# Moving the first reciprocals, the constants and the decode differences, and starting the expert products in unit 7

## The chip, the cores and the metric

The kernel runs on one core of a Trainium2 chip. A core has five engines that run their own queues in order and wait for one another by semaphores: TensorE (PE in the profile, with its weight loads as PEld), VectorE (DVE), ScalarE (ACT), GpSimd (POOL) and SyncE (SP), whose queue issues the DMAs here. The metric is the device time of one execution in microseconds, lower is better.

## The reference

Three layers follow one another on 2304 tokens (4 batches of 576) of width 512, in float32.

```python
# attention: B=4, H=8, S=576, D=64; c = cumsum(max(s, 0))
scores = q @ k.T / 8 + min(-(c_i - c_j), 0), causal      # per batch and head
attn = exp(scores - rowmax) / (rowsum + 1e-9)
x = concat_heads(attn @ v)                               # 2304 x 512
# first expert layer, d_ff = 768
x = max(max(x @ w1, x @ w2), x @ w3) @ w_out
# second expert layer, d_ff = 2048, g a rational function
h = x @ w_in
g = (a0 + a1 h + a2 h^2 + a3 h^3) / (1 + |b0| |h| + |b1| h^2 + 1e-6)
out = g @ w_out2
```

## The kernel before

**Precision.** Matmul operands of the expert layers are split into two parts: hi, a rounded copy made by ScalarE, and lo, the difference to the full value. A product is the sum of hi·hi, hi·lo and lo·hi (`mm3`, line 65): three passes over the 128-row slices, the lo weights in the last pass.

**Decode.** A 512 KB slice of a weight matrix is loaded raw, and `decode_steps` (line 416) makes hi and lo of it in five operations: three on VectorE (lines 419 to 421), which shuffle bits of the raw slice into a buffer `x` of which there is one; a cast on ScalarE to hi (line 422); and the difference on GpSimd to lo (line 423), which reads `x` and hi. The next slice's first operation writes `x` again. There are 46 such jobs: 18 slices of w1, w2, w3 (named by column group 0 to 5 and matrix 0 to 2, so (4,0) is the 13th), then 28 slices of the other weights, called sp, which are decoded in place and stored to DRAM for later ("spilled").

**Attention in units.** `units` (line 236) lists 32 units, each four heads (a group g) and one or two row tiles x. A unit passes through these stages, one or two units behind one another:
- `scores` (line 267): for four heads, three matmuls each that run side by side on 32 rows (two halves of the head dimension, then the bias). VectorE adds the mask, scales and takes the row minimum (line 291), ScalarE takes the exponential with its row sum (line 297). The last row tile (x = 3) comes in two halves.
- `norm` (line 302): VectorE adds 1e-9 to the row sums and takes reciprocals (lines 306 and 307), GpSimd multiplies each head's rows by them (line 313). `scores` schedules it two steps later.
- `transposes` of the unit before (line 328): TensorE turns the weights round, ScalarE and, for the second bank, VectorE copy them out of PSUM (lines 356 and 358).
- `pv` of two units before (line 362): the products with v; ScalarE copies the hi part of x (line 394), VectorE makes the lo part (line 395).

Score and transpose banks come from one ring of five PSUM banks.

**Fills.** As soon as a block of 384 tokens is through `pv` for all heads, its 18 expert groups (6 column groups by 3 matrices) are appended to `moe1_todo`. `fill` (line 470) issues the next one if the slice that it needs is entered in `w13`; if not, it issues nothing, and the step is spent. A group is 12 matmuls (line 72); ScalarE copies the result of matrix 0 (line 453), VectorE takes the maximum with the other two (line 455). Groups left at the end of attention run behind it.

**Order.** In this part of the program each engine's queue has the order in which the code issues. The main loop (line 541) makes a list of steps for unit u: scores, transposes, scores' second half, transposes, pv, with the fills spread between them (none before unit 8; then 3, or 4 when more than 18 groups are open or after unit 27). `step` (line 252) issues one of them, counts `now` up, takes background steps from `bg` (at least 5 behind scores) and issues what `after` has put into `late` when its step count is reached. Behind a step the loop also takes one operation from `prep`: the four VectorE transposes that turn a group's raw k and q (line 199); in unit 0 the last two of group 1, in units 7, 8, 14, 16 and so on those of a new group. A decode job is queued as `w_store`, `w_load` and `first` (line 505), and `first` puts the five operations at the head of `bg`. Line 544 gives the number of jobs that are begun by unit u:

```python
while njobs < min(len(jobs), u + max(0, u + 2 - U0) * 2 // 3):
    w_job()
```

With U0 = 8 that is 7 by unit 7, then 9, 11, 12, 14, 16, 17, 19, 21. A slice is entered in `w13` four steps behind its last decode operation's place.

**Start.** Before the loop, VectorE makes small constants `pc` from the partition number (lines 151 to 162), a selection matrix (lines 167 to 171), the scan of s (line 188), the first transposes of k and q, and from two matmuls (line 220) the tile `hx` and the bias row `cx` (line 224). GpSimd fills the mask (line 173), whose memory holds the scratch values of which `pc` is made.

After the loop come the remaining expert groups, then the second part of the kernel (lines 613 to 770), in which the spilled slices come back and the other products run.

Of the kernel before, what the change touches and what calls it, by code (L numbers as in the profile page):

```python
# [8 lines left out]
F32 = mybir.dt.float32  # L9
# [3 lines left out]
ALU = mybir.AluOpType  # L13
# [5 lines left out]
def kernel(  # L19
# [20 lines left out]
    nc = tc.nc  # L40
# [9 lines left out]
    BIG = 1000000000.0  # L50
    scale = 1.0 / float(D) ** 0.5
# [7 lines left out]
    NG = N // 4  # L59
# [40 lines left out]
    MS = 448  # L100
    mask = at.tile([128, MS], F32, name="mask")
# [7 lines left out]
    def xtile(shape, dt, name):  # L109
        return p1.tile(list(shape), dt, tag="x", bufs=3, name=name)  # L110
# [18 lines left out]
    def load_v(g):  # L129
# [12 lines left out]
    first_raw = at.tile([128, 4, S], F32, tag="PT", bufs=2, name="raw1").rearrange("p a s -> p (a s)")  # L142
    load_qk(1)

    pc = at.tile([128, 4 + 2 * NG], F32, name="pc")
    pi_ = mask.bitcast(U32)[:, 0:4 + 2 * NG]
    nc.gpsimd.iota(pi_[:, 0:1], pattern=[[0, 1]], base=0, channel_multiplier=1)
# [3 lines left out]
    nc.vector.tensor_scalar(pi_[:, 3:4], pi_[:, 0:1], 2, 7, ALU.logical_shift_right, ALU.bitwise_and)  # L153
    pf = mask[:, 32:36 + 2 * NG]
    nc.vector.tensor_copy(pf[:, 0:4 + NG], pi_[:, 0:4 + NG])
    nc.vector.tensor_copy(pc[:, 0:1], pf[:, 1:2])
    nc.vector.tensor_scalar(pc[:, 1:2], pf[:, 1:2], -2.0, 1.0, ALU.mult, ALU.add)
    nc.vector.tensor_scalar(pc[:, 2:3], pf[:, 2:3], -1.0, 1.0, ALU.mult, ALU.add)
    nc.vector.tensor_copy(pc[:, 3:4], pf[:, 2:3])
    nc.vector.tensor_scalar(pf[:, 12:12 + NG], pf[:, 4:4 + NG], pf[:, 3:4], None, ALU.is_equal)  # L160
    nc.vector.tensor_scalar(pc[:, 4:4 + NG], pf[:, 12:12 + NG], pf[:, 2:3], -1.0, ALU.mult, ALU.mult)
    nc.vector.tensor_tensor(pc[:, 4 + NG:4 + 2 * NG], pf[:, 12:12 + NG], pc[:, 4:4 + NG], ALU.add)

    wsel = xtile([128, 3, 128], F32, "wsel")
    sel, n_i = wsel[0:N, 0, :], wsel.bitcast(U32)[0:N, 1:3, :]
# [4 lines left out]
    nc.vector.tensor_copy(sel, n_i[:, 0, :])  # L170
    nc.vector.tensor_scalar(sel, sel, pf[0:N, 0:1], None, ALU.is_equal)

    nc.gpsimd.memset(mask, 0.0)
    nc.gpsimd.affine_select(
        out=mask[:, MS - 128:MS], in_=mask[:, MS - 128:MS], compare_op=ALU.is_ge,
        fill=-BIG / scale, base=0, pattern=[[-1, 128]], channel_multiplier=1)
    make_identity(nc, ident)
    for y in range(2):
        nc.gpsimd.memset(P[y][:, :, PW - 64:PW], 0.0)
# [6 lines left out]
    c = sc[:, 1, :]  # L186
    nc.vector.tensor_scalar(sc[:, 0, :], sc[:, 0, :], 0.0, 1.0 / scale, ALU.max, ALU.mult)
    nc.vector.tensor_tensor_scan(c, sc[:, 0, :], sc[:, 0, :], 0.0, ALU.add, ALU.max)


    qk_t = {}
# [21 lines left out]

    p0, p1_ = prep_qk(0), prep_qk(1)
    hx = xtile([128, 2, S], F32R, "hx")
    p0.pop(0)()
    for y in range(2):
        y0, y1 = y * S // 2, (y + 1) * S // 2
# [6 lines left out]
    for f in p0 + p1_[0:2]:  # L225
# [7 lines left out]
    USC = [[[(0, 0, 64, 0), (1, 0, 192, 64)]], [[(2, 0, 320, 0)]], [[(3, 0, 448, 0)]],  # L233
           [[(4, 0, 288, 0)], [(4, 288, 576, 0)]]]
# [14 lines left out]
    def after(lag, fn):  # L249
        late.append((now + lag, fn))  # L250

    def step(fn, *a):
        nonlocal now
        fn(*a)
        now += 1
        for _ in range(max(-(-len(bg) // bg_steps[0]), 5 if fn is scores else 0)):
            if bg:
                bg.pop(0)()
        bg_steps[0] = max(1, bg_steps[0] - 1)
        for x in [x for x in late if x[0] <= now]:  # L260
            late.remove(x)
            x[1]()

    bg = []
    bg_steps = [1]

    def scores(u, y):
        g, x = units[u]
        Pu, sm = P[u % 2], smalls[u % 3]
        kt, qt, et = qk_t["k", g], qk_t["q", g], qk_t["e", g]  # L270
        pss = [st_tile(f"sc{u}_{y}_{h}") for h in range(4)]
        for t, j0, j1, o in USC[x][y]:
            r0, nr = IT[t]
            for z in range(3):
                for h in range(4):
                    r = slice(32 * h, 32 * h + 32)
                    if z < 2:
                        l, rr = qt[r, z, r0:r0 + nr], kt[r, z, j0:j1]
                    else:
                        l, rr = et[r, r0:r0 + nr], bias_r[r, j0:j1]  # L280
                    nc.tensor.matmul(pss[h][0:nr, o:o + j1 - j0], l, rr, start=(z == 0), stop=(z == 2),  # L281
                                     tile_position=(32 * h, 0))
        for t, j0, j1, o in USC[x][y]:
            r0, nr = IT[t]
            W = r0 + nr
            base = pbase(t)
            m0 = j0 + (MS - W if nr == 128 else MS - 128) if j1 == W else 0
            last = j1 == W
            k = 4 * (t == 0)
            for h in range(4):  # L290
                nc.vector.tensor_tensor_reduce(  # L291
                    Pu[0:nr, h, base + j0:base + j1], pss[h][0:nr, o:o + j1 - j0], mask[0:nr, m0:m0 + j1 - j0], -scale,
                    3.0e38 if j0 == 0 else sm[0:nr, 3, h:h + 1], ALU.add, ALU.min,
                    sm[0:nr, 0 if last else 3, k + h:k + h + 1])
                if last:
                    o_ = Pu[0:nr, h, base:base + W]
                    nc.scalar.activation(out=o_, in_=o_, func=ACTF.Exp, bias=sm[0:nr, 0, k + h:k + h + 1], scale=-1.0,  # L297
                                         accum_out=sm[0:nr, 1, k + h:k + h + 1])
        if y == len(USC[x]) - 1:
            after(2, lambda: norm(u))  # L300

    def norm(u):
# [136 lines left out]
    w13 = {}  # L439
# [48 lines left out]
    jobs = [("w13", divmod(i, 3)) for i in range(3 * KF1)] + [("sp", x) for x in range(len(spill))]  # L488
    raws = []
    stores = []  # L490
    nj = [0]

    def w_store():
        if stores:
            o, r = stores.pop(0)
            dma.dma_start(out=o, in_=r)
# [8 lines left out]
    def w_job():  # L505

        bg.append(w_store)
        bg.append(w_load)

        def first():  # L510
            kind, x, raw = raws.pop(0)
            xx = new_wx(f"{kind}{x}")
            if kind == "w13":
                t = wslot(f"w13_{x[0]}_{x[1]}")
                args = raw, xx, t[:, 0, :], t[:, 1, :], t.bitcast(F32)[:, 0, :]
            else:
                r = raw.rearrange("p f t -> p (f t)").rearrange("p (a f) -> p a f", a=2)
                args = raw, xx, r.bitcast(F32R)[:, 0, :], r.bitcast(F32)[:, 1, :], r.bitcast(F32)[:, 0, :]
            for x_, f in enumerate(decode_steps(*args)):
                bg.insert(x_, f)  # L520
            if kind == "w13":
                bg.insert(5, lambda: after(4, lambda: w13.__setitem__((x[1], x[0]), t)))
            else:
                bg.insert(5, lambda: stores.append((w2_dram[x], r.bitcast(F32))))

        bg.append(first)

# [8 lines left out]
    U0 = 8  # L536
    nblk = 0
    njobs = 0
    prep = p1_[2:4]
    loads = []  # L540
    for u in range(NU + 2):
        g, x = units[min(u, NU - 1)]
        if u >= 1:
            while njobs < min(len(jobs), u + max(0, u + 2 - U0) * 2 // 3):
                w_job()
                njobs += 1
        nfill = 0 if u < U0 else 4 if len(moe1_todo) > 18 or u > 27 else 3
        work = []
        if u < NU:
            work += [(scores, u, 0), 1]  # L550
        if 1 <= u <= NU:
            nb = len(tr_banks(units[u - 1][1]))
            work += [(transposes, u - 1, range(2)), 1]
        if u < NU and len(USC[x]) > 1:
            work += [(scores, u, 1), 1]
        if 1 <= u <= NU:
            work.append((transposes, u - 1, range(2, nb)))
        if u >= 2:
            z = (units[u - 2][0] // 2) * S + sum(IT[UT[units[u - 2][1]][-1]])
            assert not any(t[0] <= (z - 1) // TB - 3 for t in moe1_todo)  # L560
            work.append((pv, u - 2))
        work.append(1)
        nf = sum(w == 1 for w in work)
        nfill = min(nfill, len(moe1_todo))
        seq = []
        for w in reversed(work):
            if w == 1:
                kf = -(-nfill // nf)
                nfill -= kf
                nf -= 1  # L570
                seq += [(fill, 1)] * kf
            else:
                seq.append(w)
        bg_steps[0] = len(seq)
        for i, f in enumerate(reversed(seq)):
            step(*f)
            if prep:
                prep.pop(0)()
            elif loads:
                loads.pop(0)()  # L580
        while bg:
            bg.pop(0)()
        while prep:
            prep.pop(0)()
        if u >= 2 and units[u - 2][0] % 2:
            while (nblk + 1) * TB <= z:
                moe1_todo += [(nblk, fc, m) for fc in range(KF1) for m in range(3)]
                nblk += 1
        if u == 1:
            load_qk(2)  # L590
        if u < NU and x == NX - 1 and g + 2 < NG:
            prep = prep_qk(g + 2)
            bias_l(g + 2)
            if g + 3 < NG:
                loads.append(lambda g=g: load_qk(g + 3))
        if u >= 2:
            g, x = units[u - 2]
            if x == NX - 1 and g + 2 < NG:
                load_v(g + 2)
# [50 lines left out]
    for x in range(ng):  # L650
# [4 lines left out]
        while not right and done < len(direct) and done * (ng - 6) <= (x - 5) * len(direct):  # L655
            kind, c = direct[done]
# [144 lines left out]
```

## Time and profile before

| | us |
|---|---|
| median of 3 runs | 945.13 (943.19 to 945.21) |
| profiled execution, its own time | 945.91 |
| its span, first to last instruction | 944.1 |
| TensorE busy | 902.2 (96%) |
| VectorE busy | 652.4 (69%) |
| ScalarE busy | 480.4 (51%) |
| GpSimd busy | 355.3 (38%) |

The page gives the busy time of each engine, its course in 40 slices, the DMA queues, the chain of work that ended last, and the costliest groups of instructions. A row of the timeline reads: start in us, duration of the row, engine, line of the kernel, operation, tile written and tiles read, shapes, count; in square brackets the time that the engine had stood idle before it, and what released it. Rows of the same kind that follow one another are merged. TensorE's durations overlap, since a matmul's end is modelled.

### The profile page before, as it was taken

The numbers are of one execution on the slowest core, as the hardware profiler recorded it, in microseconds if no ns is written. First come the engines' busy times: TensorE is split into PE (matmuls) and PEld (weight loads), VectorE is DVE, ScalarE is ACT, GpSimd is POOL, SyncE is SP. The second block draws the span as 40 slices with busy tenths as digits, with TensorE's granted clock in tenths as the row PEclk, the third lists the DMA queues.
The fourth block names the chain that finished last, engine by engine and source line by source line (L and its number), as shares of the span: only waits on it lengthen the run. The fifth ranks groups of instructions, "written<-read, shape, count | busy, mean of one in ns | idle before, by whom it ended". The sixth has DMA issues, their size and how long they took to land.

```text
span 944.1 us, 16698 instructions
## 1 busy us (share of the span) xinstructions
PE 902.2 (96%) x6148; PEld 808.2 (86%) x6148; DVE 652.4 (69%) x1439; ACT 480.4 (51%) x1122; POOL 355.3 (38%) x424
## 2 busy tenths in 40 slices
PE   3878999999999998999999999999999999999997
PEld 2557887898789897999999999999899989999995
DVE  7677667755676665455369859849866885885985
ACT  3655445544454443322256656546645664663764
POOL 1553443433334323132035435524533552452552
PEclk9999999999999999999999999999999999999999
DMA  8224533664467454296730020002002001000000
GB/s 248 69 68 148 157 92 116 206 210 138 151 205 212 160 171 161 85 337 201 249 134 1 1 85 1 0 1 84 1 1 84 1 1 56 29 1 1 34 1 33
DMA packets 63937, 92.90 MB, mean 98 GB/s; under 512 B 22864, under 2 KB 49488, under 8 KB 63856
## 3 DMA queue, kind: packets, MB, share of 16 engines
q1 hardware_dynamic: 63856, 91.84, 30.5%
q8 instruction: 48, 0.79, 0.4%
q14 instruction: 33, 0.27, 0.1%
HBM read 65.35 MB, written 26.48 MB: 97 GB/s over the span
## 4 chain that ended last, share of the span: by engine, by line
PE 70%; DVE 13%; POOL 7%; ACT 6%; DMA 2%; issue 2%; POOLq 0%; ACTq 0%; SPq 0%; DVEq 0%
PE m L72 21%; PE hp L72 15%; PE acc L736 14%; PE mo L72 7%; PE pv L382 5%; PE sc L281 4%; PE tr L344 4%; POOL q L706 3%; POOL q L705 2%; DVE P L291 2%; DVE q L719 2%; ACT a L717 1%; DVE t_q L199 1%; DVE t_k L199 1%; DVE t L721 1%
## 5 line engine op out<-in xcount | busy, mean ns | idle before, releaser
L72 PE MATMUL m<-x,w 128*128 128x384 f32 x1296 | 245.0, 341 | 2.1 <-DVE hs L455 1.2
L72 PEld LDWEIGHTS m<-x,w 128*128 128x128 f32 x1296 | 222.0, 188 | 12.4 <-issue 6.2
L736 PE MATMUL acc<-ws,g 128*128 128x512 f32 x864 | 217.6, 394 | 1.5 <-ACT g L722 1.5
L705 POOL TENSOR_SCALAR q<-a,cf 128x384 f32<-128x384 f32 x96 | 92.9, 968 | 289.8 <-ACT a L703 274.7
L736 PEld LDWEIGHTS acc<-ws,g 128*128 128x128 f32 x864 | 160.9, 188 | 31.0 <-ACT g L722 2.4
L313 POOL TENSOR_SCALAR P<-P,small 128x192 f32<-128x192 f32 (+4 forms) x160 | 83.2, 540 | 150.4 <-DVE small L307 130.8
L72 PE MATMUL hp<-x,w2i 128*128 128x384 f32 x720 | 134.8, 336 | 0.0
L72 PEld LDWEIGHTS hp<-x,w2i 128*128 128x128 f32 x720 | 126.6, 188 | 4.3
L297 ACT ACTIVATE P<-P,small 64x64 f32<-64x64 f32 (+4 forms) x160 | 87.9, 551 | 53.0 <-DVE small L291 52.9
L706 POOL TENSOR_TENSOR q<-q,a 128x384 f32<-128x384 f32 x96 | 104.3, 1086 | 8.0
L707 DVE TENSOR_TENSOR t<-hp,t 128x384 f32<-128x384 f32 x96 | 53.0, 552 | 57.9 <-ACT t L704 57.9
L717 ACT ACTIVATE a<-q,cf 128x384 f32<-128x384 f32 x96 | 59.3, 618 | 64.2 <-POOL q L706 64.0
L719 DVE SCALAR_TENSOR_TENSOR q<-q,cf,a 128x384 f32<-128x384 f32 x96 | 72.9, 759 | 18.0 <-ACT a L718 17.4
L344 PE MATMUL tr<-ident,P 128*128 128x128 f32 (+2 forms) x480 | 67.3, 280 | 16.6 <-POOL P L313 9.9
L722 ACT CAST g<-t 128x384 fp32r<-128x384 f32 x96 | 49.2, 513 | 65.4 <-DVE t L721 65.4
L72 PE MATMUL mo<-h,wr 128*128 128x384 f32 x432 | 79.9, 336 | 0.0
L344 PEld LDWEIGHTS tr<-ident,P 128*128 128x128 f32 (+2 forms) x480 | 54.6, 140 | 28.6 <-POOL P L313 16.3
L455 DVE TENSOR_TENSOR hs<-m,hs 128x384 f32<-128x384 f32 x72 | 39.7, 553 | 55.9 <-PE m L72 50.1
L281 PE MATMUL sc<-t_k,t_q 32*128 32x288 f32 (+4 forms) x768 | 67.2, 435 | 10.9 <-DVE t_q L199 9.0
L72 PEld LDWEIGHTS mo<-h,wr 128*128 128x128 f32 x432 | 75.6, 188 | 1.5
L291 DVE CUSTOM_DVE_ANT_0 P<-sc,mask 64x64 f32<-64x64 f32 (+4 forms) x160 | 58.8, 423 | 19.3 <-PE sc L281 19.3
L703 ACT ACTIVATE a<-hp 128x384 f32<-128x384 f32 x96 | 46.8, 488 | 36.8 <-PE hp L72 36.8
(318 smaller groups left out, 1221.4 us busy)
## 6 DMA issues: line engine op xcount, KB each, us to landing
ws<-w_dram SPq DMA_DIRECT2D x18, 512.0 KB, 4.7
h_dram<-hs SPq DMA_DIRECT2D x36, 192.0 KB, 4.1
h<-h_dram SPq DMA_DIRECT2D x36, 192.0 KB, 3.4
rb<-in_moe_w_in_dram SPq DMA_DIRECT2D x10, 512.0 KB, 5.5
wr<-w_dram SPq DMA_DIRECT2D x10, 512.0 KB, 8.0
out_dram<-o SPq DMA_DIRECT2D x18, 256.0 KB, 2.5
v<-in_v_dram SPq DMA_DIRECT2D x32, 128.0 KB, 3.9
raw_k<-in_k_dram SPq DMA_DIRECT2D x7, 576.0 KB, 3.9
```

The lines of the kernel that those rows point to most:

```text
L72: nc.tensor.matmul(ps, l, r, start=(i == 0), stop=(i == len(seq) - 1))
L281: nc.tensor.matmul(pss[h][0:nr, o:o + j1 - j0], l, rr, start=(z == 0), stop=(z == 2), tile_position=(32 * h, 0))
L291: nc.vector.tensor_tensor_reduce(Pu[0:nr, h, base + j0:base + j1], pss[h][0:nr, o:o + j1 - j0], mask[0:nr, m0:m0 + j1 - j0], -scale, 3.0e3 ...
L297: nc.scalar.activation(out=o_, in_=o_, func=ACTF.Exp, bias=sm[0:nr, 0, k + h:k + h + 1], scale=-1.0, accum_out=sm[0:nr, 1, k + h:k + h + 1])
L313: nc.gpsimd.tensor_scalar(o, o, sm[0:nr, 2, k + h:k + h + 1], 0.0, ALU.mult, ALU.add)
L344: nc.tensor.transpose(ps[0:w, o:o + nr], Pu[0:nr, h, i:i + w], ident[0:nr, 0:nr])
L705: nc.gpsimd.tensor_scalar(qq, a, cf[:, 5:6], cf[:, 4:5], ALU.mult, ALU.add)
L706: nc.gpsimd.tensor_tensor(qq, qq, a, ALU.mult)
L707: nc.vector.tensor_tensor(t, h, t, ALU.mult)
L717: nc.scalar.activation(out=a, in_=qq, func=ACTF.Ln, bias=cf[:, 6:7], scale=1.0)
L719: nc.vector.scalar_tensor_tensor(qq, qq, cf[:, 6:7], a, ALU.add, ALU.mult)
L736: nc.tensor.matmul(acc[n, tt], g[:, ga, ts], w[:, wb, :], start=(fc == 0 and x == 0), stop=(fc == KF2 - 1 and x == 2))
```

## The change

- The seven small operations that make `pc`, and GpSimd's fill of the mask, are issued behind the scan.
- The second key transpose of group 0 is issued ahead of the `hx` operations.
- `scores` takes at least 6 background steps instead of 5.
- `norm(0)` is issued in unit 0, behind the remaining `prep` transposes, instead of two steps later; the other units keep `after(2, ...)`.
- The difference, last of the five decode operations, is taken out of the list. Behind the fourth, a function `run` is put into `late` for one step later and into `flush`, which the next `w_store` empties if it comes first. `run` issues the difference and enters the slice in `w13` two steps later, or queues the store of a spilled slice.
- In unit 7, when its `pv` has completed the first block, three fill steps are added.

```diff
+    p0.pop(0)()
     p0.pop(0)()
     for y in range(2):
...
-        for _ in range(max(-(-len(bg) // bg_steps[0]), 5 if fn is scores else 0)):
+        for _ in range(max(-(-len(bg) // bg_steps[0]), 6 if fn is scores else 0)):
...
-        if y == len(USC[x]) - 1:
+        if y == len(USC[x]) - 1 and u:
             after(2, lambda: norm(u))
...
     def w_store():
+        for f in list(flush):
+            f()
         if stores:
...
-            for x_, f in enumerate(decode_steps(*args)):
+            steps = decode_steps(*args)
+            end = steps.pop()
+
+            def run():
+                if run not in flush:
+                    return
+                flush.remove(run)
+                end()
+                if kind == "w13":
+                    after(2, lambda: w13.__setitem__((x[1], x[0]), t))
+                else:
+                    stores.append((w2_dram[x], r.bitcast(F32)))
+
+            steps.append(lambda: (after(1, run), flush.append(run)))
+            for x_, f in enumerate(steps):
                 bg.insert(x_, f)
-            if kind == "w13":
-                bg.insert(5, lambda: after(4, lambda: w13.__setitem__((x[1], x[0]), t)))
-            else:
-                bg.insert(5, lambda: stores.append((w2_dram[x], r.bitcast(F32))))
...
             step(*f)
+            if u == 0:
+                while prep:
+                    prep.pop(0)()
+                norm(0)
             if prep:
...
+        if u == U0 - 1:
+            for _ in range(3):
+                step(fill, 1)
```

## Rows read from the trace of the kernel before

**Rows 1.** The page: busy us of each engine, share, instructions.

```profile
PE 902.2 (96%) x6148; PEld 808.2 (86%) x6148; DVE 652.4 (69%) x1439; ACT 480.4 (51%) x1122; POOL 355.3 (38%) x424
```

**Rows 2.** Timeline of the start: VectorE's two gaps and the second key transpose.

```profile
7.55 0.52 DVE L222 TENSOR_SCALAR hx<-c,pc 128x288 f32<-128x288 f32 x1 [0.70 <-ACT hx L221]
...
8.51 0.52 DVE L222 TENSOR_SCALAR hx<-c,pc 128x288 f32<-128x288 f32 x1 [0.44 <-ACT hx L221]
8.95 1.25 DVE L199 STREAM_TRANSPOSE t_k<-raw_k 128x576 f32<-128x576 f32 x1
```

**Rows 3.** Timeline of units 0 to 2: VectorE, ScalarE and GpSimd.

```profile
17.25 2.33 DVE L199 STREAM_TRANSPOSE t_q<-raw 128x576 f32<-128x576 f32 x2
...
18.81 0.19 ACT L297 ACTIVATION_READ_ACCUMULATOR P<-P,small 128x1 f32 x1
...
25.32 0.19 ACT L297 ACTIVATION_READ_ACCUMULATOR P<-P,small 128x1 f32 x1
25.33 5.81 POOL L313 TENSOR_SCALAR P<-P,small 128x192 f32<-128x192 f32 x16 [18.52 <-DVE small L307]
...
33.15 0.42 DVE L419 TENSOR_SCALAR w13(0, 1)x<-w13(0, 1)r 128x512 uint32<-128x512 uint32 x1
```

**Rows 4.** Timeline of units 6 to 8: normalisation, x product, first fill.

```profile
66.13 3.10 POOL L313 TENSOR_SCALAR P<-P,small 128x576 f32<-128x576 f32 x4
...
66.93 0.30 PE L344 MATMUL tr<-ident,P 128*64 128x128 f32 x1 [3.12 <-POOL P L313]
...
78.67 0.27 ACT L394 CAST x<-pv 128x128 fp32r<-128x128 f32 x1
...
79.72 2.35 PE L72 MATMUL m<-x,w 128*128 128x384 f32 x12
```

**Rows 5.** Stretches: length, busy us of PE, PEld, DVE, ACT, POOL, clock, DMA.

```profile
70.00:72.00 2.00, 2.00 (x15) 1.38 (x17) 2.00 (x4) 0.17 (x1) 0.00 (x0) 0.50 0.03 8
...
374.00:377.00 3.00, 0.20 (x2) 0.00 (x0) 2.86 (x6) 0.53 (x1) 0.00 (x0) 1.00 0.27 95
```

**Rows 6.** Chain of work that ended last: one fill, one unit's scores.

```profile
103.23 2.29 PE m L72 x12
105.52 1.39 PE sc L281 x40
```

**Rows 7.** Timeline of TensorE: first scores of units 11 to 16.

```profile
116.34 1.36 PE L281 MATMUL sc<-t_k,t_q 32*128 32x320 f32 x16
...
126.91 1.78 PE L281 MATMUL sc<-t_k,t_q 32*128 32x448 f32 x16
...
136.21 1.25 PE L281 MATMUL sc<-t_k,t_q 32*128 32x288 f32 x16
...
146.75 1.03 PE L281 MATMUL sc<-t_k,t_q 32*128 32x448 f32 x6
...
156.80 2.01 PE L281 MATMUL sc<-t_k,t_q 32*128 32x288 f32 x12
...
176.02 0.46 PE L281 MATMUL sc<-t_k,t_q 32*64 32x64 f32 x16
```

**Rows 8.** Timeline of GpSimd: differences of units 10 to 14, one normalisation.

```profile
115.12 1.28 POOL L423 TENSOR_TENSOR w<-w13(3, 2)x,w 128x512 fp32r<-128x512 f32 x1
121.88 2.07 POOL L313 TENSOR_SCALAR P<-P,small 128x320 f32<-128x320 f32 x4 [5.49 <-DVE small L307]
123.92 1.28 POOL L423 TENSOR_TENSOR w<-w13(4, 0)x,w 128x512 fp32r<-128x512 f32 x1
...
136.27 1.27 POOL L423 TENSOR_TENSOR w<-w13(4, 2)x,w 128x512 fp32r<-128x512 f32 x1
...
144.44 1.28 POOL L423 TENSOR_TENSOR w<-w13(5, 1)x,w 128x512 fp32r<-128x512 f32 x1 [2.99 <-ACT w L422]
...
158.98 1.31 POOL L423 TENSOR_TENSOR w<-w13(5, 2)x,w 128x512 fp32r<-128x512 f32 x1
```

**Rows 9.** Timeline of VectorE in unit 15: a wait for a load.

```profile
166.30 0.43 DVE L419 TENSOR_SCALAR sp1x<-sp1r 128x512 uint32<-128x512 uint32 x1 [2.54 <-DMA sp1r<-in_moe_w_out_dram]
```

More of the change, by code (lines that the diff above doesn't have):

```diff
@@ L155 @@
     nc.vector.tensor_copy(pf[:, 0:4 + NG], pi_[:, 0:4 + NG])
[L156 to L162, printed above, removed]
     wsel = xtile([128, 3, 128], F32, "wsel")
@@ L171 @@
     nc.vector.tensor_scalar(sel, sel, pf[0:N, 0:1], None, ALU.is_equal)
[L173 to L176, printed above, removed]
     make_identity(nc, ident)
@@ L188 @@
     nc.vector.tensor_tensor_scan(c, sc[:, 0, :], sc[:, 0, :], 0.0, ALU.add, ALU.max)
+    nc.vector.tensor_copy(pc[:, 0:1], pf[:, 1:2])
+    nc.vector.tensor_scalar(pc[:, 1:2], pf[:, 1:2], -2.0, 1.0, ALU.mult, ALU.add)
+    nc.vector.tensor_scalar(pc[:, 2:3], pf[:, 2:3], -1.0, 1.0, ALU.mult, ALU.add)
+    nc.vector.tensor_copy(pc[:, 3:4], pf[:, 2:3])
+    nc.vector.tensor_scalar(pf[:, 12:12 + NG], pf[:, 4:4 + NG], pf[:, 3:4], None, ALU.is_equal)
+    nc.vector.tensor_scalar(pc[:, 4:4 + NG], pf[:, 12:12 + NG], pf[:, 2:3], -1.0, ALU.mult, ALU.mult)
+    nc.vector.tensor_tensor(pc[:, 4 + NG:4 + 2 * NG], pf[:, 12:12 + NG], pc[:, 4:4 + NG], ALU.add)
+    nc.gpsimd.memset(mask, 0.0)
+    nc.gpsimd.affine_select(
+        out=mask[:, MS - 128:MS], in_=mask[:, MS - 128:MS], compare_op=ALU.is_ge,
+        fill=-BIG / scale, base=0, pattern=[[-1, 128]], channel_multiplier=1)
     qk_t = {}
@@ L490 @@
     stores = []
+    flush = []
     nj = [0]
     def w_store():
+        for f in list(flush):
+            f()
         if stores:
```

## The prediction

> **What bounds the kernel now.** I read the page's engine line first: TensorE is busy 96% of the span [rows 1], so the kernel can gain or lose only by time in which TensorE stands still, 42 us in all. Three views then show where it stands. The timeline of the start: up to the first scores TensorE waits for VectorE, and VectorE itself has two gaps of 0.70 and 0.44 us [rows 2]. The timeline of units 0 to 2 (I count units from 0, so the "eighth unit" is unit 7): GpSimd idles until 25.33 us and then normalises units 0 and 1 together, 16 operations in 5.81 us [rows 3]; from there a loop of normalisation, decode difference, the next slice's decode and the next reciprocals runs over VectorE and GpSimd up to unit 6. Unit 7 is the last starved one: TensorE stands still for 3.12 us before the transposes at 66.93 [rows 4]. From unit 8 on, expert groups ("fills", 12 matmuls, 2.28 us on the chain of waits [rows 6]) fill the gaps.
>
> **The start: -1.2 us.** The seven small pc operations go behind the scan. The scan starts earlier, but VectorE's first key transpose comes where it was, since the same work stands ahead of it. What changes is the next step: the second key transpose (1.25 us) runs while the matmuls and copies are made for which VectorE had waited, so the gaps of 0.70 and 0.44 go [rows 2]. The mask's fill on GpSimd now waits for pc; its first reader is unit 0's reduction, behind the scores, so that costs nothing. Bounds: 0 if the gaps reappear behind the transposes, 1.3; I take 1.2, the gaps themselves.
>
> **First reciprocals: -2.8 us.** Unit 0's exponentials end at 19.00 and VectorE's query transposes at 19.58 [rows 3]. The two small operations fit there with no wait, ahead of unit 1's reductions, which wait for unit 1's scores; were the exponentials later, the reductions would now wait behind them. GpSimd then does unit 0's half (2.9 us) at about 20. Unit 1's half waits for its own exponentials, which end at 25.51, less the 1.2 of the start: 24.3; with 0.6 for the reciprocals GpSimd runs from 24.9 to 27.8 instead of to 31.1. The difference of slice (0,0) (1.3 us, as those in [rows 8]) ends at 29.1. What is late next is the decode of slice (0,1): it writes the buffer that this difference reads, so it starts at 29.15 instead of 33.15. Start and reciprocals together thus give 4.0, and the loop carries them on. Bounds: 1.2 and 5.2 (GpSimd's first operation moves from 25.33 to 20.1).
>
> **Sixth background step, late difference.** In units 1 to 5 GpSimd's order stays the same (normalisation, then the difference), so nothing is gained. The third decode step stands ahead of VectorE's copy of the transposes instead of behind it: under 0.7 us each, on a copy that is not on the loop; 0. In unit 6 the order turns: the normalisation at 66.13 stood behind a difference of 1.3 us [rows 4, 8], and now stands ahead of it. But the next slice's decode on VectorE waits for that difference, with unit 7's reductions and four transposes queued behind, and VectorE sets unit 7. I take the two as cancelling. The stores of spilled slices are queued with their difference, at the latest at the next store step, so SP's order is kept: 0, or one step on a transfer that these units do not read.
>
> **Three fills in unit 7: +1.0 us.** They need the x products, whose copy was at 78.67 [rows 4] and comes, by the order of ScalarE and VectorE, within 0.6 us of that (less the 4.0). Before, unit 8's scores ran in this hole and the first fill began at 79.72. Now TensorE stands still (about 3.4 us), the fills follow at 79.3 and end at 86.0, and the scores (1.4 us, [rows 6]) end at 87.4. Less three fills (6.7) that is 80.7 against 79.7. Bounds: 0 if the copy comes 1 us sooner, +4 with rival 2 below.
>
> **What the lead costs later: +9.1 us.** Total fills before the end of unit 20 are the same by the loop's rules, 39; the lead of three is given back in units 11 (one fill instead of three), 15 and 20, with unit 14 at two instead of one. The reason is the decode: 12 slices are through by unit 10, and with the lead the 13th fill needs slice (4,0), decoded in unit 11 itself. The new lag is three steps, and steps whose fill is not ready take no time. So TensorE meets the difference on GpSimd, which is queued behind the unit's normalisation, and next unit's scores are queued behind the fill. Scores, reductions, decode, normalisation, difference, fill become one serial loop:
> - Unit 10: the difference of (3,2) ends at 116.40 [rows 8], about when the old last fill ended (scores of 11 at 116.34, [rows 7]). Its last third needs it: +0.8.
> - Unit 11: the difference of (4,0) ends at 125.20 [rows 8], 8.9 after the unit's scores [rows 7]; with the fill's last third (0.75) 9.6 us. Before 10.6 with two fills more (4.6): +3.6.
> - Unit 12: the difference of (4,2) ends 10.6 after the scores [rows 7, 8]. With 0.75, less 0.3 for a decode that is earlier, 11.1 against 9.3, two fills each: +1.8.
> - Unit 13: 10.5 before. The first fill is missed; the first transposes wait for reductions behind a whole decode (1.1), and the second half of the scores for a PSUM copy queued on ScalarE behind a cast, which waits for the slice behind the 1.3 us difference [rows 8] (1.6); with small ones 13.7: +3.2.
> - Unit 14: the difference of (5,2) ends 13.5 after the scores [rows 7, 8], some 2 less where these run unstalled; with 0.75 and one more fill 14.5 against 10.05, less 2.3: +2.2.
> - Unit 15: before 19.2 with four fills [rows 7], VectorE waiting 2.54 for a load [rows 9] that stood in SP's queue behind a query load; now it is issued ahead of that. About 14.4, TensorE's own work with three fills: -2.5.
>
> The sum of these is 9.1. Bounds: -0.3 (unit lengths of 11 to 14 kept, with one fill less, and the 2.5 of unit 15) and 12 (no gain in 15). I take the trace's own intervals. A rule speaks to the same place: the Trainium skill, "TensorE: Matmul & The Clock Gate", "Step-by-step: what each phase is for", says that "the MATMULs themselves stay in program order", only weight loads being pulled ahead. By that rule the scores cannot pass a fill that waits, and the 9.1 stands; were they able to, it would be -0.3. The trace agrees: the transposes at 66.93 held everything behind them for 3.12 us [rows 4].
>
> After unit 20 the order is that of before. **Sum:** -1.2 - 2.8 + 1.0 + 9.1 = +6.1. The profiled execution took 945.91; it becomes 952.0, and on the scale of the median (945.13, 0.8 lower) **951.2**.
>
> **Rivals.**
> 1. Faster: VectorE and GpSimd set the length of units 11 to 14 in both kernels, and TensorE reaches each slice no earlier than its difference. Then the later cost is -0.3: -1.2 - 2.8 + 1.0 - 0.3 = -3.3, 941.8. For it: the chain of unit 14 (13.5 us) was longer than the unit (10.05) before, too [rows 7, 8]. Against: unit 11 took 10.6 us with the difference done at 8.9 [rows 7, 8], so there TensorE was the bound. It decides at a wait of TensorE below 0.5 us per unit in 11 to 14.
> 2. The clock falls in unit 7's new hole. After the 3.12 us still stand and sparse transposes the granted clock was 0.50, the 1.2 GHz level, over 70 to 72 us; after 2.8 still us of 374 to 377 it stayed at 1.00, 2.4 GHz [rows 4, 5]. At half clock the fills lose a second 2.28 us each until it returns, some 3 us: 954.2. The Trainium skill, same page, "What's actually happening", has the throttled state as the default that activity releases, which is why a hole ahead of dense work could cost twice.
> 3. A wash: the stalls are half as long as I trace them (4.5 instead of 9.1) and the start keeps its whole 5.2: -5.2 + 1.0 + 4.5 = +0.3, 945.4.
>
> **How the numbers follow.** The forecast gets 0.50 (own range 947 to 955), rival 2 0.16, rival 1 0.22, rival 3 0.12. About 0.2% (1.9 us) is what a measurement can tell from no change: faster 0.22, within 0.12, slower 0.66. The range reaches over rival 1 down to 940.5, and to 958 for rival 2 with every stall: 940.5 to 958.
>
> **What would show it.** First scores 1.2 us earlier; normalisation of unit 0 near 19 to 20, slice (0,1)'s decode near 29; three fills in unit 7 behind a still TensorE; TensorE waiting for GpSimd's w in fills of units 10, 11, 12 and 14, a wait that the list of before does not have. I am wrong if those waits are missing, or if the lead of some 3 us at unit 9 is still there at unit 16.

## The result, and the profile after

The changed kernel took 957.0 us (median) where the kernel before took 945.2: ratio 1.0123, 95% interval [1.0100, 1.0146]. A second set of runs gave 954.0 against 946.0, 1.0081 [1.0057, 1.0104]. So it is slower by 8 to 12 us. One of the first set's four runs, the profiled one, took 1014.3 us at a mean granted clock of 0.85; the ratio leaves it out (the other three have a median of 956.8), and the lines of "after" come from the second set's profile (955.59 us, span 953.8, clock 0.996). Its line numbers from 218 to 488 are one higher than before: L345 is the transpose, L424 the decode difference.

The page's engine line, to be set beside [rows 1]: no engine got more work. The span grew by 9.7 us, and TensorE's busy time by 1.3.

```profile
PE 903.5 (95%) x6148; PEld 807.4 (85%) x6148; DVE 653.6 (69%) x1439; ACT 480.2 (50%) x1122; POOL 352.8 (37%) x424
```

The start, VectorE and then GpSimd: the two key transposes now follow each other without the gaps of [rows 2]; normalisation of unit 0 begins at 19.13 instead of 25.33, and the decode of slice (0,1) at 29.26 instead of 33.15 [rows 3].

```profile
6.09 2.33 DVE L199 STREAM_TRANSPOSE t_k<-raw_k 128x576 f32<-128x576 f32 x2
8.26 0.86 DVE L223 TENSOR_SCALAR hx<-c,pc 128x288 f32<-128x288 f32 x2
...
29.26 0.43 DVE L420 TENSOR_SCALAR w13(0, 1)x<-w13(0, 1)r 128x512 uint32<-128x512 uint32 x1 [1.96 <-POOL w L424]
```

```profile
19.13 2.77 POOL L314 TENSOR_SCALAR P<-P,small 128x192 f32<-128x192 f32 x8 [12.06 <-DVE small L308]
25.21 2.77 POOL L314 TENSOR_SCALAR P<-P,small 128x192 f32<-128x192 f32 x8 [3.32 <-DVE small L308]
27.96 1.26 POOL L424 TENSOR_TENSOR w<-w13(0, 0)x,w 128x512 fp32r<-128x512 f32 x1
```

TensorE in units 7 to 14, from the rows in which it waited (before: [rows 4, 7]). 74.10 to 81.3 are the three early fills of unit 7; before, the first fill began at 79.72. From 119.32 on, each row but one is a fill that waits for its slice: for GpSimd's difference (POOL w) or ScalarE's rounding (ACT w).

```profile
68.95 1.97 PE L345 MATMUL tr<-ident,P 128*128 128x128 f32 x8 [2.21 <-DVE PT L357]
74.10 0.62 PE L72 MATMUL m<-x,w 128*128 128x384 f32 x2 [0.83 <-ACT PT L359]
75.23 6.17 PE L72 MATMUL m<-x,w 128*128 128x384 f32 x34 [0.51 <-ACT x L395]
...
119.32 0.97 PE L72 MATMUL m<-x,w 128*128 128x384 f32 x4 [0.69 <-POOL w L424]
125.97 1.69 PE L72 MATMUL m<-x,w 128*128 128x384 f32 x8 [1.43 <-ACT w L423]
129.10 0.96 PE L72 MATMUL m<-x,w 128*128 128x384 f32 x4 [1.44 <-POOL w L424]
...
140.31 0.96 PE L72 MATMUL m<-x,w 128*128 128x384 f32 x4 [1.21 <-POOL w L424]
...
148.18 0.77 PE L282 MATMUL sc<-t_k,t_q 32*128 32x288 f32 x8 [0.65 <-DVE PT L357]
...
165.60 3.08 PE L72 MATMUL m<-x,w 128*128 128x384 f32 x16 [3.01 <-POOL w L424]
```

The list of TensorE's waits between 92 and 260 us, first of the kernel before, then of the changed one (us in total, times, longest). The second has two rows on slices (w), 7.7 us together, and the first has none.

```profile
PE tr L344 <- DVE small L291: 1.6, 2, 1.0
PE m L72 <- DVE hs L455: 1.2, 1, 1.2
PE sc L281 <- ACT PT L358: 1.0, 1, 1.0
PE tr L344 <- POOL P L313: 0.4, 1, 0.4
```

```profile
PE m L72 <- POOL w L424: 6.3, 4, 3.0
PE tr L345 <- DVE small L292: 2.1, 3, 1.0
PE m L72 <- ACT hs L454: 1.8, 1, 1.8
PE m L72 <- ACT w L423: 1.4, 1, 1.4
PE sc L282 <- DVE PT L357: 0.7, 1, 0.7
...
```

A measure used below is the **lag** of a kernel behind the one before: the start of a unit's x products (pv) in its timeline, less the same start before, less 2.22 us for each fill that it has done more by then. For the changed kernel the lag is -4.4 us in unit 2, -4.8 in unit 7, -3.8 in unit 10, -2.4 in unit 11, +1.3 in unit 12, +5.1 in unit 13, +4.3 in unit 15, +6.2 in unit 19 and +9.4 in unit 31. From the lead of 4.8 in unit 7 to the lag of 9.4 in unit 31 it loses 14.2 us, and 8.9 of them arise between the pv of unit 10 and that of unit 13. A lag is read from one execution, and the executions of one kernel spread by about 1 to 6 us.

### The profile page after: what moved, and what is told of

It reads as the page before. It is cut to its first block, busy times and chain, and to the rows that moved or that the text cites. A ratio compares the mean times of both kernels' runs of the same rounds, so it can differ in the third digit from the quotient of the medians.

```text
span 1012.5 us, 16683 instructions
## 1 busy us (share of the span) xinstructions
PE 974.5 (96%) x6148; PEld 855.2 (84%) x6148; DVE 650.8 (64%) x1439; ACT 483.2 (48%) x1122; POOL 353.2 (35%) x424
## 4 chain that ended last, share of the span: by engine, by line
PE 89%; DVE 7%; POOL 2%; issue 1%; DMA 1%; ACT 0%; POOLq 0%; SPq 0%; DVEq 0%; ACTq 0%
PE m L72 23%; PE hp L72 21%; PE acc L757 21%; PE mo L72 8%; PE sc L282 6%; PE pv L383 5%; PE tr L345 4%; DVE P L292 2%; POOL P L314 1%; POOL w L424 1%; DVE t_k L199 1%; DVE t_q L199 1%; DMA rb<-in_moe_w_in_dram 1%; DVE PT L357 0%; ACT P L298 0%
## 5 line engine op out<-in xcount | busy, mean ns | idle before, releaser
L72 PE MATMUL m<-x,w 128*128 128x384 f32 x1296 | 264.9, 360 | 8.9 <-POOL w L424 5.1
L72 PEld LDWEIGHTS m<-x,w 128*128 128x128 f32 x1296 | 237.6, 193 | 22.0 <-issue 6.7
L757 PE MATMUL acc<-ws,g 128*128 128x512 f32 x864 | 234.1, 416 | 0.0
L757 PEld LDWEIGHTS acc<-ws,g 128*128 128x128 f32 x864 | 165.1, 192 | 38.9
L72 PE MATMUL hp<-x,w2i 128*128 128x384 f32 x720 | 145.4, 354 | 0.0
L72 PEld LDWEIGHTS hp<-x,w2i 128*128 128x128 f32 x720 | 135.2, 192 | 6.7
L72 PE MATMUL mo<-h,wr 128*128 128x384 f32 x432 | 86.3, 354 | 0.0
L345 PE MATMUL tr<-ident,P 128*128 128x128 f32 (+2 forms) x480 | 74.2, 297 | 10.5 <-DVE small L292 4.3
L72 PEld LDWEIGHTS mo<-h,wr 128*128 128x128 f32 x432 | 80.9, 192 | 2.5
L345 PEld LDWEIGHTS tr<-ident,P 128*128 128x128 f32 (+2 forms) x480 | 58.2, 145 | 26.9 <-POOL P L314 10.0
```

The costliest lines, as they stand in the source:

```text
L72: nc.tensor.matmul(ps, l, r, start=(i == 0), stop=(i == len(seq) - 1))
L345: nc.tensor.transpose(ps[0:w, o:o + nr], Pu[0:nr, h, i:i + w], ident[0:nr, 0:nr])
L757: nc.tensor.matmul(acc[n, tt], g[:, ga, ts], w[:, wb, :], start=(fc == 0 and x == 0), stop=(fc == KF2 - 1 and x == 2))
```

## The experiments

My theory after the result was that the lead of three fills costs what the prediction said. I took the change apart.

**The changed kernel again, and without the fills.** The second is the changed kernel less these lines:

```diff
-        if u == U0 - 1:
-            for _ in range(3):
-                step(fill, 1)
```

> The changed kernel once more, for a trace whose clock can be compared with the one of before. Serial-loop theory (the lead of three fills brings TensorE up to the decode): about 957 us, TensorE waits for GpSimd's lo halves in units 10 to 14, 5 us or more in all, and units 11 to 14 take together about 49 us instead of 40.5. Clock theory: the granted clock is 0.50 during unit 7's fills and this costs 3 us or more there. Late-difference theory (the late subtraction itself holds VectorE's decode): VectorE waits for GpSimd before the decode's first operation more than before, in units 1 to 10 already.

> The changed kernel without the three fills in unit 7; all else of the change stays. Serial-loop theory: faster than before by the 4.0 us of the start and the reciprocals, 941 us (939.5 to 943), with no waits for lo halves. Late-difference theory: still slower than before, 950 or more. If the fills cost only their hole and the clock (4 us), about 953.

Measured: 954.0, and 950.9 without the fills (1.0056 [1.0036, 1.0077]). Units 11 to 14 took 48.4 us (scores of unit 11 at 120.22, of unit 15 at 168.60) against 40.5 before. The fills carry about 3 us of the loss; without them the kernel is still 5 us slower than before, although it starts 4.9 us ahead in its trace.

**The fills alone, and the late difference together with the sixth step.** The first adds those three lines to the kernel before. The second is the kernel before with `flush` and `run` of the change and six steps instead of five.

> The kernel before with only the three fill steps in unit 7; the difference stays in its old place, a slice is usable four steps behind it. Serial-loop theory: TensorE still comes up to the decode in unit 10 or 11 (by the loop's rules units 10 and 11 have two and one fill instead of three and three), and it costs what it cost in the changed kernel or a little less: 945 + 1 + 6 to 12 = 952 to 958. Late-difference theory: about 946, as the early differences keep their place.

> The kernel before with only the late difference (run, flush, usable two steps later) and the sixth background step. Serial-loop theory: no lead, so no serial loop: 945 us within 1.5. Late-difference theory: 950 us or more.

Measured: 948.0 (1.0019 [1.0009, 1.0029]) and 955.8 (1.0104 [1.0085, 1.0122]). The theory of the lead fell: the fills with five steps cost 2.1 us, and the loss comes without any lead. Next I had to part the late difference from the sixth step.

**The sixth step alone.** The kernel before with one figure changed:

```diff
-        for _ in range(max(-(-len(bg) // bg_steps[0]), 5 if fn is scores else 0)):
+        for _ in range(max(-(-len(bg) // bg_steps[0]), 6 if fn is scores else 0)):
```

> The kernel before with only the sixth background step behind scores (decode operations stay five in a row). Order theory (the late difference costs, by VectorE's wait for the one decode buffer and by the store that a raw buffer's next load waits for): within 1.5 us of before. Sixth-step theory (the third decode step holds VectorE's copy of the transposes, and with it a PSUM bank): slower by 5 us or more.

**The late difference alone**, with five steps: for the expert slices only (`if kind == "w13"` chooses between `run` and the old order), and for the spilled slices only (`kind == "sp"`).

> The kernel before with the late difference only for the 18 slices of w1, w2, w3, with five background steps. Order theory: about +4 us (3 to 6), lost in units 6 to 15, where VectorE's decode waits for the difference behind the normalisation; nothing later. Sixth-step theory: within 2 us of before.

> The kernel before with the late difference only for the 28 spilled slices, with five background steps. Order theory: about +4 us (3 to 6), all of it behind unit 15: the store starts later, the load into the same raw buffer behind it, and VectorE waits for that load (5 us for sp7). Sixth-step theory: within 2 us of before.

Measured: the sixth step 956.6, 1.0120 [1.0103, 1.0136], as slow as the whole change; the late difference 946.1 (1.0002 [0.9990, 1.0013]) and 946.8 (1.0010 [0.9997, 1.0023]), no difference. One figure carries the loss.

**The start alone**: the moved pc and mask lines, the second key transpose ahead, and

```diff
+            if u == 0:
+                while prep:
+                    prep.pop(0)()
+                norm(0)
```

> The kernel before with only the start of the change: constants and mask behind the scan, second key transpose ahead, reciprocals of unit 0 in unit 0. All theories: faster by 4 to 5 us, 941; the prediction's terms say 4.0, the pair of runs without and with it (950.9 against 955.8) 4.9. If the lead is taken back later by the clock or by the loads, 943 to 946.

Measured: 943.4, 0.9969 [0.9957, 0.9980]. It is the only gain in the change. Its lag is -4.4 us in unit 2 and still -4.2 in unit 21: what the start wins is kept up to there; in unit 31 the lag is -3.4. That trace is of a quick run (941.8). The median lies in the range expected of a lead that is taken back in part, and where the other runs lose it is not known.

**Where the sixth step costs.** With six steps alone the lag is -0.1 in unit 12, +6.4 in unit 13, +8.1 in unit 15 and +11.2 at the end. ScalarE's timeline of unit 13, in the kernel before and then with the sixth step (CAST w is the fourth decode step, COPY PT empties the score bank that held the transposes):

```profile
140.41 0.53 ACT L358 COPY PT<-tr 128x448 f32<-128x448 f32 x1 [0.30 <-PE tr L344]
143.74 0.62 ACT L422 CAST w<-w13(5, 1)x 128x512 fp32r<-128x512 f32 x1 [2.80 <-DVE w13(5, 1)x L421]
```

```profile
143.27 0.62 ACT L422 CAST w<-w13(5, 1)x 128x512 fp32r<-128x512 f32 x1 [3.29 <-DVE w13(5, 1)x L421]
143.79 0.52 ACT L358 COPY PT<-tr 128x448 f32<-128x448 f32 x1
```

The copy and the cast have changed places. The score step now issues all three VectorE steps of slice (5,1), so the next step issues the cast ahead of the transposes and their copy. The cast cannot start before VectorE has decoded the slice, and the copy that was done at 140.94 is done at 144.31. Five banks go round; unit 13 takes four for its first scores, two for the transposes, and its second scores need the transposes' first bank back. Three of the four heads go ahead without it (x6 in the row of 140.55, two records a matmul), and the fourth waits. TensorE with the sixth step, and its stretches (columns as in [rows 5]):

```profile
140.55 1.08 PE L281 MATMUL sc<-t_k,t_q 32*128 32x288 f32 x6
144.28 1.34 PE L281 MATMUL sc<-t_k,t_q 32*128 32x288 f32 x8 [2.65 <-DVE PT L356]
```

```profile
141.00:143.00 2.00, 0.63 (x6) 0.17 (x2) 1.58 (x3) 0.00 (x0) 0.32 (x1) 1.00 0.66 235
...
145.00:149.00 4.00, 4.00 (x21) 3.21 (x14) 1.84 (x8) 1.77 (x5) 0.22 (x1) 0.50 0.45 146
149.00:151.00 2.00, 2.00 (x9) 1.90 (x8) 0.35 (x2) 1.40 (x5) 0.01 (x1) 0.50 0.00 0
151.00:153.00 2.00, 2.00 (x32) 1.83 (x30) 0.00 (x0) 1.43 (x3) 2.00 (x3) 0.99 0.00 0
```

The wait is put down to VectorE's copy, which ends a hair before these scores go on (ScalarE's ends 0.03 us after that, by the records). But that copy stands at 143.62 in both kernels, and before, these scores ran from 140.68 without a wait. Only ScalarE's copy moved. TensorE and VectorE before, then VectorE with the sixth step:

```profile
140.68 1.24 PE L281 MATMUL sc<-t_k,t_q 32*128 32x288 f32 x12
143.62 0.62 DVE L356 COPY PT<-tr 128x448 f32<-128x448 f32 x1
```

```profile
143.62 0.61 DVE L356 COPY PT<-tr 128x448 f32<-128x448 f32 x1
```

The hole is 2.65 us, and then the granted clock is 0.50, the 1.2 GHz level, for more than 6 us, worth some 3 us more: about 6 together, and the lag rose by 6.5. At 164.7 it falls to half once more, behind unit 14, which has no fill left since unit 13 took one more. Over 128 to 180 us, taken in stretches of 1 us, TensorE stood 3.6 us (before 2.8) and lost 6.7 us to the clock (before 0).

**Is it this place, and does six or five decide the changed kernel too?** Four kernels: six steps at the first scores of unit 13 only; six everywhere but in unit 13; the changed kernel with five; the start alone with four. Of the first two edits only the part of the line that changes is shown.

```diff
-  5 if fn is scores else 0
+  (6 if a == (13, 0) else 5) if fn is scores else 0
...
-  5 if fn is scores else 0
+  (5 if a[0] == 13 else 6) if fn is scores else 0
```

> Kernel before, with six background steps behind one call alone, the first score step of unit 13; everywhere else five. Theory 'rounding ahead of the copy': there the sixth step puts ScalarE's rounding of slice (5,1) in front of the copy that frees the score bank, so the second score step of unit 13 waits (2.65 us in the trace with six steps everywhere) and TensorE then runs at half clock for some 6.6 us (about 3.3 us lost); and since unit 13 then takes one expert group more, unit 14 has none and a second half-clock stretch of about 6.4 us (3.2 us) may follow. Sum about +8 us: 952 to 955, where before is 945.9. Rival 'every score step pays a little' (10.7 us over some 40 score steps, 0.27 us each): 946.2, no difference.

> The complement: six background steps behind every score step but the two of unit 13, which keep five. Theory 'rounding ahead of the copy': what is left of the 10.7 us is what came outside units 13 to 15, about 2.6 us: 947 to 949.5. Rival 'every score step pays a little': about 956, as with six everywhere.

> The changed kernel with five background steps instead of six and nothing else altered: new start, late differences, three expert products in unit 7. If the parts add up as measured alone (start -2.5, products +2.1, late difference +0.2 to +0.9): 945.5 to 947, no more than 0.2% from before; the sixth step then carries the whole loss. Rival 'the lead costs': with the start ahead the expert products stand still further ahead of their slices and the waits on GpSimd's differences stay (6 us in the changed kernel's trace): 950 to 952.

> The new start alone (943.4 when it was run) with four background steps behind a score step instead of five. Order of expert products unchanged. If five was already enough to keep the rounding behind the copy, as the first theory has it, four changes little: 942.5 to 944.5. If each decode step placed ahead of the copies and reductions costs by itself, four gains again: 940 to 942. If the slices come too late with four: 945 or more, with longer waits for GpSimd's differences.

Measured: unit 13 alone 952.1 (1.0064 [1.0048, 1.0081]). One call out of some 40 costs 6.2 us, so "every score step pays a little" is out. The lag is 0.0 in unit 12 and +4.9 in unit 13. The wait of 2.65 us is there (up to 144.39), and the half clock behind it costs 1.7 us more; the second half-clock stretch that I expected did not come.

Six everywhere but in unit 13: 953.7 (1.0085 [1.0070, 1.0100]), where I expected at most 949.5. A miss: the place is not the only one. Its lag is -0.1 from unit 8 to unit 14 and +5.1 in unit 15, the next unit with two score steps, where ScalarE and TensorE show the same picture:

```profile
168.10 0.62 ACT L422 CAST sp1r<-sp1x 128x512 fp32r<-128x512 f32 x1 [5.20 <-DVE sp1x L421]
168.63 0.52 ACT L358 COPY PT<-tr 128x448 f32<-128x448 f32 x1
```

```profile
169.12 1.34 PE L281 MATMUL sc<-t_k,t_q 32*128 32x288 f32 x8 [2.97 <-DVE PT L356]
```

```profile
170.00:174.00 4.00, 4.00 (x18) 3.21 (x15) 2.51 (x10) 1.93 (x5) 0.06 (x1) 0.50 0.71 187
```

Before, the copy stood at 162.81, and these scores ran from 165.38 without a wait:

```profile
162.81 0.53 ACT L358 COPY PT<-tr 128x448 f32<-128x448 f32 x1
```

```profile
165.38 1.25 PE L281 MATMUL sc<-t_k,t_q 32*128 32x288 f32 x16
```

The mechanism held where the count of places did not. The two partial kernels' losses (6.2 and 7.8) add to more than 10.7: with six in both units, TensorE waits only 0.8 us at the scores of unit 15, and mainly the clock costs there.

The changed kernel with five steps: 947.3 (1.0015 [1.0002, 1.0029]), just above what the parts add up to (945.5 to 947), so the sixth step is worth 6.7 to 9.7 us of the changed kernel's time too. There it works mainly by other waits: the exchange of cast and copy is there with six steps (in unit 13, cast at 147.62 and copy at 148.15), but costs only the 0.65 us of the row at 148.18. The list of the kernel with five for the same stretch (from its quickest run, 943.3 of 943.3 to 949.3, so the list is on the low side):

```profile
PE tr L345 <- DVE small L292: 3.7, 4, 1.0
PE m L72 <- POOL w L424: 1.9, 1, 1.9
PE m L72 <- ACT w L423: 1.1, 1, 1.1
...
```

Waits for slices fall from 7.7 to 3.0 us. By the loop's rules a slice that is through decoding one step sooner is ready for a fill one step sooner: the fills of (3,2), (4,0) and (4,2) stand at the end of units 10, 11 and 12 with six steps, and behind the next unit's scores with five. The TensorE rows of 119.32 to 140.31 shown above are these three fills, and none of them has a wait with five.

The start with four steps: 941.0, 0.9947 [0.9933, 0.9962], the fastest of all. That lies in the range of "each decode step costs by itself" (940 to 942), not in that of the first theory (942.5 to 944.5). The bank's copy stays ahead of the cast in it, as with five (in unit 13 at 137.04 and 140.76), and TensorE's wait for hs (1.0 us with five) is gone. Whether four beats five with the same start is not settled: the two were timed in different sets, and their intervals overlap a little.

## Why the prediction was right, and where it was not

It forecast 951.2 in 940.5 to 958; the time was 957.0, and 954.0 in the second set.

- **Start and first reciprocals**, -4.0: the trace has -4.4 in unit 2 and -4.8 in unit 7. Right; the times named (19 to 20, 29) are those seen. The shares differ: the first scores begin 1.65 us earlier (10.34 for 11.99), but unit 0's reductions only 0.9 (14.65 for 15.55), and the reciprocals gave the rest. Alone the start is worth 2.5 us in the medians.
- **Three fills in unit 7**, +1.0: the lag went from -4.8 to -3.7. Right, though TensorE stood in other places than I drew: 2.21 us ahead of the transposes and 1.3 at the fills, instead of 3.4 in one piece. Rival 2 did not happen in this kernel: the fills ran from 74 to 81 at a granted clock of 1.00. In the two kernels with these fills and five steps it did: there TensorE stood 3.30 us (fills alone) and 3.49 us (changed, five steps) in one piece, as I had drawn it, and the clock was 0.50 over 78 to 81 and over 74 to 77.
- **What the lead costs later**, +9.1: the waits came where they were named, on GpSimd's difference in fills of units 10, 11, 12 and 14. By the lag unit 10 cost 1.4 (0.8 forecast), unit 11 3.7 (3.6), unit 12 3.8 (1.8), unit 13 -1.1 (3.2), units 14 and 15 together 0.3 (-0.3): 8.1 for 9.1. Unit 12 was 2.0 too low and unit 13 4.3 too high, so that the sum came out is in part luck. TensorE indeed did not take the scores past a waiting fill: the scores of unit 12 begin at 129.99, only behind the fill that waits at 129.10. Rival 1 needed waits under 0.5 us and is out.
- **After unit 20 the order is that of before**, 0: wrong in size. Units 16 to 20 lost another 2.2 us (the largest wait between 180 and 260 is 1.79 us for hs, at 222.65) and units 21 to 31 another 2.9. About 1.5 of these are the clock in unit 31: all kernels have a hole of 2.6 to 3.7 us there (before at 374 [rows 5]), but before, the clock stayed at 1.00 behind it, and here its mean was 0.57 over 386 to 390. The rest goes with the sixth step too: between units 15 and 30 the lag of the five kernels that have it throughout, or everywhere but in unit 13, grows by 2.0 to 5.5 us, and that of the seven others by no more than 1.2 (from -1.0). By which waits it does so stays open.
- **"Sixth background step … under 0.7 us each, on a copy that is not on the loop; 0"**: this is the step that failed. I looked only at VectorE's copy. The step also pulls ScalarE's cast in front of ScalarE's copy, and it makes each slice ready one step earlier. Alone it costs 10.7 us, and with it gone the lead costs little: with five steps the lag moves by 2.4 us from unit 9 to unit 15 (-3.4 to -1.0, in the trace of its quickest run), with six by 8.1 (-3.8 to +4.3). My +9.1 was put on the lead, but it needs both. I even named the copy "queued on ScalarE behind a cast" in unit 13, and charged it to the lead.
- The **late difference**, cancelling: 0.2 and 0.9 us, within what can be told from none. Right.

So the direction, the range and the place of the loss were right, the sum was 3 to 6 us short, and its largest term stood under the wrong edit. That the time still fell into the range, with the edit that decides the outcome put at 0, is partly luck.

## What to carry over

When work is handed out in steps, a change of how many steps follow a call changes the order on every engine that the later steps belong to; list for each engine which instruction now stands ahead of which, and ask what each waits for. An instruction with a long wait must not stand ahead of one that frees a buffer TensorE needs. And before trusting a term of the sum, ask which single edit would make it vanish.

## What was not expected of the hardware

Holes of like length did not have like consequences for the clock. After 2.65 us (six steps) the granted clock was 0.50 for more than 6 us, after 2.65 us in the kernel with six steps in unit 13 only, for about 3; after 3.01 us in the changed kernel it stayed at 1.00:

```profile
163.00:165.00 2.00, 0.00 (x0) 0.00 (x0) 2.00 (x3) 0.00 (x0) 2.00 (x4) 1.00 0.70 234
165.00:167.00 2.00, 1.40 (x8) 1.40 (x9) 1.17 (x3) 0.00 (x0) 0.55 (x1) 1.00 0.47 141
```

In the first two, scores (32 rows a tile) ran ahead of the hole and behind it; in the changed kernel both neighbours were fills, 128 by 128. But that does not decide it either. In the kernel before with the late difference and six steps, a hole of 3.00 us between fills was followed by half clock for about 3 us (a mean of 0.57 over the 4 us shown):

```profile
164.85 4.49 PE L72 MATMUL m<-x,w 128*128 128x384 f32 x16 [3.00 <-POOL w L423]
```

```profile
164.00:168.00 4.00, 3.15 (x10) 3.15 (x11) 2.45 (x5) 0.00 (x0) 0.80 (x1) 0.57 0.65 222
```

In the changed kernel without its early fills, a hole of 3.00 us between fills (up to 159.26) left the clock at 1.00. What decides it stays open.
